# RWKV scan and MoE rewritten as 64-token chunks of two batches on array halves, with the MoE woven into the scan

## The chip, the cores and the metric

The kernel runs on one core of one Trainium2 chip. The metric is the device time of one execution in microseconds (us), lower is better. The kernel before takes 1229.74 us, median of 3 runs (1228.9 to 1230.77).

PE is TensorE's matmul side (PEld its weight load), DVE is VectorE, ACT ScalarE, POOL GpSimd, SP SyncE, which here only issues DMAs. Each engine works through its own queue in order. A "unit" below is 128 rows: 64 tokens of two batches. A "turn" is one pass of the changed kernel's main loop, which finishes one unit.

## The reference, cut to what matters

```python
# batch 4, 8 heads, 768 tokens, head size 40; state is 40 x 40 per batch and head
for t in range(S):
    y[:, :, t] = einsum('bhd,bhde->bhe', rt, state)
    Sa = einsum('bhde,bhe->bhd', state, at)
    state = state * wt[:, :, None, :] - einsum('bhd,bhe->bhde', Sa, bt) \
            + einsum('bhd,bhe->bhde', vt, kt)
x = y.transpose(0, 2, 1, 3).reshape(3072, 320)
h = x @ w_in                                   # 320 x 2048
g = where(h > 0, h, exp(minimum(h, 0)) - 1)    # ELU
out = g @ w_out                                # 2048 x 320
```

The recurrence over tokens can be done by chunks: inside a chunk it is matrix products with triangular masks and a triangular solve; only the 40 x 40 state passes from chunk to chunk.

## The kernel before

It has two stages. The scan takes 6 chunks of 128 tokens and in each handles 32 pairs of batch and head one after the other; the MoE takes the result in groups of 512 tokens.

```python
for c in range(NC):                      # 6 chunks
    ...                                  # load r k v w a b of the chunk, Ln, cumulative sum, Exp
    for bh in range(BH):                 # 32 batch-head pairs
        def transp(x_slice, name, dt=BF16):
            pT = psL.tile([D, C], FP32, name="pT", tag="psL")
            nc.tensor.transpose(pT, x_slice, id128)          # fp32
            xA = phA.tile([D, C], dt, name=name, tag="phA")
            nc.vector.tensor_copy(xA, pT)
            return xA
        r_A = transp(r_S[:, bh, :], "r_A")
        ...                              # v, ktil, atil, cw
        pU = php.tile([C, D], FP32, name="pU", tag="php")
        nc.tensor.matmul(pU, atil_A, s_ed_b, start=True, stop=False)
        nc.tensor.matmul(pU, Kd, v_b[:, bh, :], start=False, stop=True)
        nc.vector.tensor_copy(U_Sf, pU)
        U_A = transp(U_Sf, "U_A")
        ...                              # two masked products, y, state update
...
for gi in range(NG):                     # 6 groups of 512 tokens
    ...
    for j in range(NFB):                 # 16 blocks of 128 features
        ...                              # 3 matmuls into ph
        nc.vector.tensor_scalar(hneg, ph, scalar1=0.0, scalar2=None, op0=ALU.min)
        nc.scalar.activation(hneg, hneg, AF.Exp)
        nc.vector.tensor_scalar(hneg, hneg, scalar1=-1.0, scalar2=None, op0=ALU.add)
        nc.vector.tensor_scalar(g, ph, scalar1=0.0, scalar2=None, op0=ALU.max)
        nc.vector.tensor_add(gT, g, hneg)
        ...                              # 4 matmuls into oacc
```

Of the kernel before, what the change touches and what calls it, by code (L numbers as in the profile page):

```python
# [8 lines left out]
FP32 = mybir.dt.float32  # L9
AF = mybir.ActivationFunctionType  # L10
ALU = mybir.AluOpType


@with_exitstack
def kernel(
    ctx: ExitStack,
    tc: tile.TileContext,
    r: bass.AP,
    k: bass.AP,
    v: bass.AP,  # L20
    w: bass.AP,
    a: bass.AP,
    b: bass.AP,
    moe_w_in: bass.AP,
    moe_w_out: bass.AP,
    out: bass.AP,
):
    nc = tc.nc
    B, H, S, D = r.shape
    BH = B * H  # L30
    C = 128
    NC = S // C
    dmod = H * D
    dff = moe_w_in.shape[1]
    ntok = B * S

    x_tmp = nc.dram_tensor("rwkv_y", (ntok, dmod), FP32, kind="Internal").ap()

    const = ctx.enter_context(tc.tile_pool(name="const", bufs=1))
    id128 = const.tile([128, 128], FP32, name="id128")  # L40
    nc.gpsimd.memset(id128, 0.0)
    nc.gpsimd.affine_select(id128, id128, pattern=[[-1, 128]], channel_multiplier=1,
                            base=0, compare_op=ALU.not_equal, fill=1.0)
    tri_li = const.tile([128, 128], FP32, name="tri_li")
    nc.gpsimd.memset(tri_li, 1.0)
    nc.gpsimd.affine_select(tri_li, tri_li, pattern=[[1, 128]], channel_multiplier=-1,
                            base=0, compare_op=ALU.is_ge, fill=0.0)
    mask_sl = const.tile([128, 128], FP32, name="mask_sl")
    nc.gpsimd.memset(mask_sl, 1.0)
    nc.gpsimd.affine_select(mask_sl, mask_sl, pattern=[[1, 128]], channel_multiplier=-1,  # L50
                            base=-1, compare_op=ALU.is_ge, fill=0.0)

    st_pool = ctx.enter_context(tc.tile_pool(name="state", bufs=1))
    state_de = st_pool.tile([D, BH, D], FP32, name="state_de")
    state_ed = st_pool.tile([D, BH, D], FP32, name="state_ed")
    nc.gpsimd.memset(state_de, 0.0)
    nc.gpsimd.memset(state_ed, 0.0)

    def view(t):
        return t.rearrange("b h (nc s) d -> nc s b h d", s=C)  # L60
    rV, kV, vV, wV, aV, bV = [view(t) for t in (r, k, v, w, a, b)]
    xV = x_tmp.rearrange("(b nc s) (h d) -> nc s b h d", b=B, nc=NC, h=H)

    BF16 = mybir.dt.bfloat16
    rwkv_ctx = ExitStack()
    chS = rwkv_ctx.enter_context(tc.tile_pool(name="chS", bufs=2))
    tmpS = rwkv_ctx.enter_context(tc.tile_pool(name="tmpS", bufs=1))
    phA = rwkv_ctx.enter_context(tc.tile_pool(name="phA", bufs=16))
    php = rwkv_ctx.enter_context(tc.tile_pool(name="php", bufs=6, space=bass.MemoryType.PSUM))
    psL = rwkv_ctx.enter_context(tc.tile_pool(name="psL", bufs=2, space=bass.MemoryType.PSUM))  # L70

    for c in range(NC):
        r_S = chS.tile([C, BH, D], FP32, name="r_S")
        k_S = chS.tile([C, BH, D], FP32, name="k_S")
        v_S = chS.tile([C, BH, D], FP32, name="v_S")
        w_S = chS.tile([C, BH, D], FP32, name="w_S")
        a_S = chS.tile([C, BH, D], FP32, name="a_S")
        b_S = chS.tile([C, BH, D], FP32, name="b_S")
        for tS, tV in [(r_S, rV), (k_S, kV), (v_S, vV), (w_S, wV), (a_S, aV), (b_S, bV)]:
            nc.gpsimd.dma_start(out=tS.rearrange("s (b h) d -> s b h d", b=B),  # L80
                                in_=tV[c])

        F = BH * D
        lw = tmpS.tile([C, BH, D], FP32, name="lw")
        nc.scalar.activation(lw, w_S, AF.Ln)
        cw = tmpS.tile([C, BH, D], FP32, name="cw")
        lwf = lw.rearrange("s b d -> s (b d)")
        cwf = cw.rearrange("s b d -> s (b d)")
        nn = 0
        while nn < F:  # L90
            step = min(512, F - nn)
            pcs = psL.tile([C, step], FP32, name="pcs", tag="psL")
            nc.tensor.matmul(pcs, tri_li, lwf[:, ds(nn, step)], start=True, stop=True)
            nc.vector.tensor_copy(cwf[:, ds(nn, step)], pcs)  # L94
            nn += step
        Wpre = tmpS.tile([C, BH, D], FP32, name="Wpre")
        nc.vector.tensor_sub(Wpre, cw, lw)
        nc.scalar.activation(Wpre, Wpre, AF.Exp)
        necw = tmpS.tile([C, BH, D], FP32, name="necw")
        nc.scalar.activation(necw, cw, AF.Exp, scale=-1.0)  # L100
        ktil = tmpS.tile([C, BH, D], FP32, name="ktil")
        nc.vector.tensor_mul(ktil, k_S, necw)
        nbtil = tmpS.tile([C, BH, D], FP32, name="nbtil")
        nc.vector.tensor_mul(nbtil, b_S, necw)
        nc.scalar.mul(nbtil, nbtil, -1.0)
        atil = tmpS.tile([C, BH, D], FP32, name="atil")
        nc.vector.tensor_mul(atil, a_S, Wpre)

        y_S = chS.tile([C, BH, D], FP32, name="y_S")

        v_b = tmpS.tile([C, BH, D], BF16, name="v_b"); nc.vector.tensor_copy(v_b, v_S)
        ktil_b = tmpS.tile([C, BH, D], BF16, name="ktil_b"); nc.vector.tensor_copy(ktil_b, ktil)
        nbtil_b = tmpS.tile([C, BH, D], BF16, name="nbtil_b"); nc.vector.tensor_copy(nbtil_b, nbtil)

        for bh in range(BH):
            def transp(x_slice, name, dt=BF16):
                pT = psL.tile([D, C], FP32, name="pT", tag="psL")
                nc.tensor.transpose(pT, x_slice, id128)  # L118
                xA = phA.tile([D, C], dt, name=name, tag="phA")
                nc.vector.tensor_copy(xA, pT)  # L120
                return xA
            r_A = transp(r_S[:, bh, :], "r_A")
            v_A = transp(v_S[:, bh, :], "v_A")
            ktil_A = transp(ktil[:, bh, :], "ktil_A")
            atil_A = transp(atil[:, bh, :], "atil_A")
            cw_A = transp(cw[:, bh, :], "cw_A", FP32)

            s_de = state_de[:, bh, :]
            s_ed = state_ed[:, bh, :]
            s_de_b = phA.tile([D, D], BF16, name="s_de_b", tag="phA")  # L130
            nc.vector.tensor_copy(s_de_b, s_de)
            s_ed_b = phA.tile([D, D], BF16, name="s_ed_b", tag="phA")
            nc.vector.tensor_copy(s_ed_b, s_ed)

            pKd = php.tile([C, C], FP32, name="pKd", tag="php")
            nc.tensor.matmul(pKd, ktil_A, atil_A, start=True, stop=True)  # L136
            Kd = phA.tile([C, C], BF16, name="Kd", tag="phA")
            nc.vector.tensor_mul(Kd, pKd, mask_sl)  # L138
            pU = php.tile([C, D], FP32, name="pU", tag="php")
            nc.tensor.matmul(pU, atil_A, s_ed_b, start=True, stop=False)  # L140
            nc.tensor.matmul(pU, Kd, v_b[:, bh, :], start=False, stop=True)  # L141
            U_Sf = phA.tile([C, D], FP32, name="U_Sf", tag="phA")
            nc.vector.tensor_copy(U_Sf, pU)  # L143
            U_S = phA.tile([C, D], BF16, name="U_S", tag="phA")
            nc.vector.tensor_copy(U_S, pU)
            U_A = transp(U_Sf, "U_A")
            pA1 = php.tile([C, C], FP32, name="pA1", tag="php")
            nc.tensor.matmul(pA1, v_A, r_A, start=True, stop=True)
            A1 = phA.tile([C, C], BF16, name="A1", tag="phA")
            nc.vector.tensor_mul(A1, pA1, mask_sl)  # L150
            pA2 = php.tile([C, C], FP32, name="pA2", tag="php")
            nc.tensor.matmul(pA2, U_A, r_A, start=True, stop=True)  # L152
            A2 = phA.tile([C, C], BF16, name="A2", tag="phA")
            nc.vector.tensor_mul(A2, pA2, mask_sl)
            pY = php.tile([C, D], FP32, name="pY", tag="php")
            nc.tensor.matmul(pY, r_A, s_de_b, start=True, stop=False)
            nc.tensor.matmul(pY, A1, ktil_b[:, bh, :], start=False, stop=False)
# [10 lines left out]
            nc.tensor.matmul(pSd, s_ed, id128[:D, :D], start=True, stop=True)  # L168
            nc.vector.tensor_copy(s_de, pSd)

        nc.gpsimd.dma_start(out=xV[c], in_=y_S.rearrange("s (b h) d -> s b h d", b=B))

    rwkv_ctx.close()

# [6 lines left out]
    KM = [128, 128, 64]  # L181
    FB = 128
# [83 lines left out]
```

## Time and profile before

| | scan | MoE |
|---|---|---|
| until | about 940 us | 1229 us |
| PE busy, DVE busy | 76%, 76% (200 to 800 us) | 73%, 91% (1000 to 1200 us) |
| granted TensorE clock | 0.51 | 0.82 |

These are the lines of the windows view: a stretch in us, its length, the busy time of each engine with the number of instructions, the granted clock as a share of full speed, the DMA share and GB/s.

```profile
200.00:800.00 600.00, 457.30 (x2295) 207.92 (x2294) 454.97 (x2183) 51.99 (x147) 27.78 (x17) 0.51 0.09 20
1000.00:1200.00 200.00, 146.91 (x570) 55.04 (x578) 181.86 (x377) 46.63 (x74) 20.54 (x38) 0.82 0.10 32
```

In the scan no engine is full, because PE and DVE wait for each other inside each small problem. This group of the profile's page (line, engine, operation, output from input, count, busy us, mean ns, idle time before it and what ended most of it) shows one such wait, 192 times:

```profile
L118 PE MATMUL pT<-id_58,U_Sf 128*40 128x128 f32 x192 | 76.9, 401 | 56.3 <-DVE U_Sf L143 56.3
```

In the MoE DVE is the bound. The timeline shows its four ops on PSUM or SBUF per block of 128 x 512 (start, duration):

```profile
1152.12 0.68 DVE L226 TENSOR_SCALAR g<-ph 128x512 f32<-128x512 f32 x1
1152.72 0.42 DVE L224 TENSOR_SCALAR hneg<-hneg 128x512 f32<-128x512 f32 x1
1153.05 0.68 DVE L222 TENSOR_SCALAR hneg<-ph 128x512 f32<-128x512 f32 x1
1153.65 0.68 DVE L228 TENSOR_TENSOR gT<-g,hneg 128x512 bf16<-128x512 f32 x1
```

They repeat every 2.13 us.

### The profile page before, as it was taken

How to read it: one execution, taken by the hardware profiler on the slowest of the kernel's cores; microseconds unless marked ns; L12 is line 12 of the kernel's file. 1: busy time of each engine (PE TensorE's matmuls, PEld its weight loads, DVE VectorE, ACT ScalarE, POOL GpSimd, SP SyncE). 2: the span in 40 equal slices, each digit the busy share in tenths (PEclk: the TensorE clock that was granted, in tenths of full speed). 3: DMA queues.
4: the chain of work that ended last, by engine and by line, in shares of the span. 5: the costliest groups of instructions: out<-in, count | busy, mean ns of one | idle time of the engine just before them, and what ended most of it. 6: DMA issues, size and time to landing. Idle time of an engine off the chain costs nothing. (4 is left out here: it accounts for less than half of the span.)

```text
span 1229.1 us, 13572 instructions
## 1 busy us (share of the span) xinstructions
PE 883.8 (72%) x4224; PEld 387.0 (31%) x4236; DVE 935.9 (76%) x3823; ACT 144.9 (12%) x324; POOL 111.7 (9%) x121
## 2 busy tenths in 40 slices
PE   1688876888768886688867888688883567776774
PEld 0233332333323333333323333233331122222221
DVE  1877777777777777777777777777774789889986
ACT  1200011000110001100011000100000122222221
POOL 5400012000120001100010000000002210110010
PEclk9555555555555555555555555555555589779888
DMA  8920024000240002300020000000003310110000
GB/s 144 181 39 1 1 65 86 1 1 1 65 86 1 1 1 65 64 1 1 1 65 1 1 1 1 22 1 1 1 1 122 102 43 1 43 43 21 23 33 22
DMA packets 10713, 41.51 MB, mean 34 GB/s; under 512 B 1744, under 2 KB 1744, under 8 KB 10320
## 3 DMA queue, kind: packets, MB, share of 16 engines
q0 software_dynamic: 10640, 40.64, 14.6%
q8 instruction: 33, 0.54, 0.2%
q14 instruction: 40, 0.33, 0.1%
HBM read 32.77 MB, written 7.86 MB: 33 GB/s over the span
## 5 line engine op out<-in xcount | busy, mean ns | idle before, releaser
L164 ACT ACTIVATE Wall<-cw_A 40x1 f32<-40x1 f32 x192 | 39.0, 203 | 768.0 <-DVE cw_A L120 754.8
L118 PE MATMUL pT<-id_58,ktil 128*40 128x128 f32 x192 | 77.1, 402 | 58.6 <-DVE r_A L120 41.2
L118 PE MATMUL pT<-id_58,U_Sf 128*40 128x128 f32 x192 | 76.9, 401 | 56.3 <-DVE U_Sf L143 56.3
L120 DVE CAST U_A<-pT 40x128 bf16<-40x128 f32 x192 | 54.3, 283 | 74.5 <-PE pT L118 74.5
L223 ACT ACTIVATE hneg<-hneg 128x512 f32<-128x512 f32 x96 | 60.5, 630 | 221.2 <-DVE hneg L222 184.7
L143 DVE COPY U_Sf<-pU 128x40 f32<-128x40 f32 x192 | 38.3, 200 | 61.7 <-PE pU L141 61.7
L118 PE MATMUL pT<-id_58,cw 128*40 128x128 f32 x192 | 80.5, 419 | 0.8 <-DVE ktil_A L120 0.8
L118 PE MATMUL pT<-id_58,r_S 128*40 128x128 f32 x192 | 80.4, 419 | 0.3 <-DVE cw L94 0.3
L118 PE MATMUL pT<-id_58,atil 128*40 128x128 f32 x192 | 76.9, 400 | 4.7 <-DVE v_A L120 4.6
L118 PE MATMUL pT<-id_58,v_S 128*40 128x128 f32 x192 | 76.8, 400 | 0.4 <-DVE cw L94 0.2
L120 DVE CAST atil_A<-pT 40x128 bf16<-40x128 f32 x192 | 54.3, 283 | 26.2 <-PE pT L118 0.5
L136 PE MATMUL pKd<-atil_A,ktil_A 40*128 40x128 bf16 x192 | 50.5, 263 | 30.1 <-DVE atil_A L120 30.1
L222 DVE TENSOR_SCALAR hneg<-ph 128x512 f32<-128x512 f32 x96 | 65.8, 685 | 8.3 <-PE ph L219 8.2
L168 PE MATMUL pSd<-id_58,state_ed 40*40 40x40 f32 x384 | 67.6, 274 | 0.8 <-DVE state_ed L166 0.4
L226 DVE TENSOR_SCALAR g<-ph 128x512 f32<-128x512 f32 x96 | 65.7, 684 | 0.0
L228 DVE TENSOR_TENSOR gT<-g,hneg 128x512 bf16<-128x512 f32 x96 | 65.4, 682 | 0.1
L138 DVE TENSOR_TENSOR Kd<-pKd,mask_sl 128x128 bf16<-128x128 f32 x192 | 62.6, 326 | 0.0
L140 PE MATMUL pU<-s_ed_b,atil_A 40*128 40x40 bf16 x192 | 36.2, 188 | 35.1 <-DVE Kd L138 10.6
L230 PEld LDWEIGHTS <-gT 128*128 128x128 bf16 x384 | 32.6, 104 | 86.6 <-DVE gT L228 71.9
L152 PEld LDWEIGHTS <-U_A 40*128 40x128 bf16 x192 | 19.3, 101 | 126.5 <-DVE U_A L120 119.0
L80 POOL DMA_DIRECT2D r_S<-in_r_dram x6 | 10.3, 1713 | 502.6 <-PE pT L118 239.7
L120 DVE CAST ktil_A<-pT 40x128 bf16<-40x128 f32 x192 | 54.3, 283 | 2.0 <-PE pT L118 1.5
(2089 smaller groups left out, 1891.2 us busy)
## 6 DMA issues: line engine op xcount, KB each, us to landing
r_S<-in_r_dram POOLq DMA_DIRECT2D x6, 640.0 KB, 7.2
k_S<-in_k_dram POOLq DMA_DIRECT2D x6, 640.0 KB, 8.0
v_S<-in_v_dram POOLq DMA_DIRECT2D x6, 640.0 KB, 8.7
w_S<-in_w_dram POOLq DMA_DIRECT2D x6, 640.0 KB, 10.6
a_S<-in_a_dram POOLq DMA_DIRECT2D x6, 640.0 KB, 9.6
b_S<-in_b_dram POOLq DMA_DIRECT2D x6, 640.0 KB, 10.5
rwkv_y<-y_S POOLq DMA_DIRECT2D x6, 640.0 KB, 3.7
x_t<-rwkv_y POOLq DMA_DIRECT2D x24, 160.0 KB, 2.5
```

The source lines that it names most:

```text
L118: nc.tensor.transpose(pT, x_slice, id128)
L120: nc.vector.tensor_copy(xA, pT)
L136: nc.tensor.matmul(pKd, ktil_A, atil_A, start=True, stop=True)
L138: nc.vector.tensor_mul(Kd, pKd, mask_sl)
L140: nc.tensor.matmul(pU, atil_A, s_ed_b, start=True, stop=False)
L143: nc.vector.tensor_copy(U_Sf, pU)
L164: nc.scalar.activation(Wall, cw_A[:, C - 1:C], AF.Exp)
L168: nc.tensor.matmul(pSd, s_ed, id128[:D, :D], start=True, stop=True)
L222: nc.vector.tensor_scalar(hneg, ph, scalar1=0.0, scalar2=None, op0=ALU.min)
L223: nc.scalar.activation(hneg, hneg, AF.Exp)
L226: nc.vector.tensor_scalar(g, ph, scalar1=0.0, scalar2=None, op0=ALU.max)
L228: nc.vector.tensor_add(gT, g, hneg)
```

## The change

The intent: handle all 8 heads of two batches in one unit of 64 tokens, so that one eviction serves 16 small products; put the two batches on two halves of the array, rows and columns 0 to 63 and 64 to 127, so that neighbouring small matmuls don't meet; solve the triangular system (I + N) x = f with a few products by N and N squared, with a check on the chip that N squared is small and a general branch for when it is not; and weave the MoE of an earlier unit into the scan of a later one, by hand, so that no engine has to wait. The file is new almost throughout; this is its core:

```diff
-    for c in range(NC):
-        ...
-        for bh in range(BH):
-            ...                     # one head at a time
-    for gi in range(NG):
-        ...                         # MoE afterwards
+        self.ld = P("ld", 5)        # w k a b, fp32
+        self.vn = P("vn", 6)        # v, bf16
+        self.wk = P("wk", 4, space=psum)
+    def diag(self):
+        for h in range(8):
+            for bb in range(2):     # the two batches alternate
+                yield h, slice(64*bb, 64*bb+64), slice(64*bb, 64*bb+40), h == 0, h == 7
+    def load(self, n):
+        ...                         # w k a b by the SP queue, 8 runs of 160 bytes per partition
+        x = self.vn.tile([128, 8, 40], BF16, name="vn")
+        for bb in range(2):         # fp32 -> bf16 in the DMA, by the POOL queue
+            self.nc.gpsimd.dma_start(out=x[...], in_=self.v[...])
+    def ln(self, n):   ...          # ACT Ln
+    def winv(self, n): ...          # ACT Exp
+    def mulA(self, n):
+        self.nc.gpsimd.tensor_mul(self.Ap[n % 3][:, :, 0:40], self.live["a", n], self.live["wpre", n])
+    def ds(self, n):                # state update, reads vn of unit n
+        for h, tb, fb, first, last in self.diag():
+            self.mm(o, K[tb, h, :], V[tb, h, :], first, False)
+            self.mm(o, B[tb, h, :], U[tb, h, 0:40], False, last)
+        ...
+        for n in range(-3, NU + 4):             # one turn
+            if n >= -1:
+                do(self.load, n + 5)
+            ...                                 # in two turns of four: r and v for the transposes
+            do(self.elu2, n - 3, 2)
+            do(self.xt, n - 2)
+            ...
+            do(self.mulA, n + 2)                # POOL
+            ...
+            do(self.elu1, n - 2, 0, nc.gpsimd)  # ELU half on POOL
+            do(self.x1, n)
+            do(self.ut, n - 1)
+            do(self.ds, n - 1)
+            do(self.ntr, n + 1)
+            do(self.ln, n + 3)
+            do(self.trAK, n + 2)                # PE transposes of Ap and Kp
+            ...
+        return nc.values_load(self.flag, min_val=0, max_val=1)
+    with tc.manual_schedule():
+        more = Chunks(own, tc, *args).run()
+        with tc.If(more > 0):
+            Chunks(own, tc, *args).general()
```

## The prediction

> **What bounds the kernel now.** Two stages in series. In the windows view the scan runs to about 940 us and the MoE from about 945 to 1229 us. The scan handles 6 chunks x 32 heads = 192 small problems, 4.9 us each; in 200 to 800 us PE and DVE are each busy 76%: neither is full, because they wait on each other (groups: PE waits 56 us for U_Sf). The granted clock there is 0.51. In the MoE DVE is the bound (182 us busy of 1000 to 1200 us), five ops per 128x512 block, 2.1 us per block in the timeline, clock 0.8. ACT is busy 12%.
>
> **What the change does.** It runs scan and MoE together: 24 units of 128 rows (64 tokens x two batches), the MoE of unit n-2 woven into the scan of later units, so 945 us and 284 us overlap. All eight heads share one PSUM bank, so one 128x512 or 128x320 eviction replaces 16 small ones (DVE pays 0.28 us for 40x128, 0.68 us for 128x512 out of PSUM). fp32 transposes (0.19 us start to start in the timeline) become bf16. The round trip of y and the fp32 weight casts (no PE work at 945 to 962 us) go. It adds a solve in N and N-squared steps, a certificate and a general branch; computed from the inputs, the certificate is 0.00085 against a limit of 0.00195, so the branch is not taken.
>
> **Cost of one unit (estimates).**
> - PE: 352 small matmuls (40 or 64 columns), 48 of 128 columns, 16 of 320, 4 others. Before, with a 40-column load and matmul each, start to start was 0.05 to 0.06 us at clock 0.5; 320 columns took 0.135 us at full clock. The Trainium skill (TensorE: Matmul & The Clock Gate, Part 3) says a weight load overlaps a matmul in flight only where the row group differs, which alternating the two batches on two halves gives (not shown here yet). So I take 0.03 to 0.04 us per small matmul: 12.5 us; plus 3.3 (48), 2.2 (16), 0.8, and about 1 us of mode changes. Sum about 19 us, range 15 to 27.
> - DVE: ops of 0.68 us and some of 0.4: about 10 us.
> - ACT: 0.63 us per 512 elements: four exps, evictions, the square: about 10 us, plus two table loads of 1.28 us if Ln and Exp still alternate (the trace shows 12 loads in 6 chunks): 12 us.
> - POOL: multiplies, state update, two ELU ops, descriptors: 8 to 11 us.
> - DMA: before moved 640 KB of 160-byte runs per 3.6 us; a unit needs 7 to 8 us.
>
> So PE bounds a unit, at 16 to 20 us if waits are hidden and the clock nears 1. 24 x 17.5 us = 420 us, plus about 60 us for filling and draining: 480 us.
>
> **What would show it.** Clock above 0.85 in the middle; PE busy over 85%, ACT 60 to 75%, DVE 50 to 65%; a period of 16 to 20 us per unit; small matmuls 0.03 to 0.04 us start to start; two table loads per unit.
>
> **What would make it wrong.** (1) The clock stays at half although PE is dense: a unit takes 28 us or more, 700 us in all. (2) Small matmuls don't overlap (0.055 us): 600 us. (3) ACT's in-order queue stalls the solve's chain of five evictions per unit. (4) POOL runs late with its ELU half. (5) A unit takes 13 us: 370 us.
>
> Predicted 480 us, 390 to 620; faster 0.97, same 0.02, slower 0.01.

## The result and the profile after

The changed kernel takes 507.77 us, median of 4 runs (505.85 to 509.45), against 1230.26 us of the kernel before in the same rounds. The ratio is 0.4127, 95% interval 0.4117 to 0.4138. Ratios here are the mean time of one kernel's fast runs over that of the other's of the same rounds, so not quite the ratio of the medians. The output is correct and the general branch did not run.

The prediction said 480 us, 390 to 620: right in the time. Its parts were not all right, and the trace shows that at once. The busy times of the page (part 1):

```profile
PE 343.3 (68%) x9948; PEld 283.3 (56%) x9948; DVE 221.5 (44%) x465; ACT 288.7 (57%) x504; POOL 256.9 (51%) x254
```

Per unit (divided by 24) this is 9.2 us for DVE, 12.0 for ACT and 10.7 for POOL, as estimated. But no engine is near full, PE least of all as forecast ("PE busy over 85%"). The timeline of PE shows why (start, duration with the pipeline's latency, count; the distance between starts is what PE really spends):

```profile
157.46 0.41 PE L346 MATMUL wkb<-idb,STb 40*64 40x40 bf16 x16
157.72 0.42 PE L45 MATMUL wkf<-RT,VT 40*64 40x64 bf16 x16
157.97 0.42 PE L45 MATMUL wkf<-RT,UT 40*64 40x64 bf16 x16
158.63 0.44 PE L202 MATMUL wkb<-idb,Bp 64*64 64x64 bf16 x16 [0.24 <-DVE S L213]
159.00 0.84 PE L45 MATMUL h<-xT,win 128*128 128x128 bf16 x12
159.68 0.71 PE L45 MATMUL po<-wout,g 128*128 128x320 bf16 x4
160.32 0.43 PE L45 MATMUL wkf<-xs,N2T 64*64 64x40 bf16 x16
```

Most groups of sixteen small matmuls take 0.26 us, 0.016 us each; the prediction had 0.03 to 0.04. With 0.68 us for 12 matmuls of 128 columns and 0.64 us for 4 of 320, PE's own work is 352 x 0.016 + 4 x 0.68 + 4 x 0.64 + about 0.8 = about 12 us per unit, not 19. (That is an estimate from this stretch, where PE runs at its full rate.) Yet a turn takes 17.2 us, and 20.7 us in the two turns of four that also load r and v for the transposes (distance between the starts of the xT copies on ACT). The waits view (who waited for whom, us in total, times, longest) says where the rest is:

```profile
PE wkb L202 <- POOL Ap L184: 96.6, 20, 16.8
DVE g L413 <- POOL t L407: 91.7, 32, 6.7
POOL vn L129 <- PE wkb L238: 76.3, 16, 5.6
```

PE waits 97 us for POOL's multiply Ap; and POOL waits 76 us, before a DMA issue for vn, for PE. POOL's timeline over one turn (in brackets the idle time before, and what ended it):

```profile
262.80 1.46 POOL L129 DMA_DIRECT2D vn<-in_v_dram  x2 [4.70 <-PE wkb L238]
264.25 0.89 POOL L184 TENSOR_TENSOR Ap<-na,wpre 128x320 bf16<-128x320 f32 x1
265.09 1.94 POOL L407 TENSOR_SCALAR t<-e 128x512 bf16<-128x512 f32 x1
266.99 0.73 POOL L337 TENSOR_TENSOR S<-t,WTr 128x320 f32<-128x320 f32 x1
271.22 1.02 POOL L178 TENSOR_TENSOR Kp<-nk,winv 128x320 bf16<-128x320 f32 x1 [3.50 <-ACT winv L162]
272.37 1.92 POOL L407 TENSOR_SCALAR t<-e 128x512 bf16<-128x512 f32 x1
274.25 1.02 POOL L181 TENSOR_TENSOR Bp<-nb,winv 128x320 bf16<-128x320 f32 x1
280.00 1.46 POOL L129 DMA_DIRECT2D vn<-in_v_dram  x2 [4.73 <-PE wkb L238]
```

POOL is idle 8 us of 17: 3.5 us of them it waits for ACT's winv, and 4.7 us it stands at the vn issue, with Ap and the rest of its queue behind it. That load is for unit n+5, and the tile vn has 6 buffers, so it overwrites unit n-1, which the state update `ds(n-1)` still reads in the middle of the same turn. The releaser that the profile names is the matmul group right behind `ds` on PE. So there is a loop: `ds` on PE releases the load, the load releases Ap, Ap releases the transposes, and PE goes on from there to the next `ds`. Every item on it adds to the turn; the r and v issues (four, 3.6 us together in this trace) stand between vn and Ap and match the 3.5 us between the two kinds of turns.

Where the span of 503.7 us goes: the first xT copy starts at 84.9 us, the last at 482.5 us (23 distances, 17.3 us on average, the first 17 of them 19.1 us; the last turns have less and less to do), and 21.2 us follow. Fill and drain are longer than the 60 us that were forecast.

### The profile page after: what moved, and what is told of

The parts are those of the page before. It is cut to its first block, busy times and chain, and to the rows that moved or that the text cites. A ratio compares the mean times of both kernels' runs of the same rounds, so it can differ in the third digit from the quotient of the medians.

```text
span 503.7 us, 22017 instructions
## 1 busy us (share of the span) xinstructions
PE 343.3 (68%) x9948; PEld 283.3 (56%) x9948; DVE 221.5 (44%) x465; ACT 288.7 (57%) x504; POOL 256.9 (51%) x254
## 2 busy tenths in 40 slices
DMA packets 210743, 36.05 MB, mean 72 GB/s; under 512 B 205200, under 2 KB 210320, under 8 KB 210640
## 3 DMA queue, kind: packets, MB, share of 16 engines
q0 software_dynamic: 77680, 8.53, 29.9%
## 5 line engine op out<-in xcount | busy, mean ns | idle before, releaser
L407 POOL TENSOR_SCALAR t<-e 128x512 bf16<-128x512 f32 x48 | 92.8, 1934 | 44.6 <-ACT e L401 21.6
L413 DVE TENSOR_TENSOR g<-t,h 128x512 bf16<-128x512 bf16 x96 | 65.5, 682 | 93.7 <-POOL t L407 91.7
L45 PE MATMUL h<-xT,win 128*128 128x128 bf16 x1152 | 91.2, 236 | 2.3 <-DVE g L413 2.2
L129 POOL DMA_DIRECT2D vn<-in_v_dram x48 | 35.0, 736 | 87.5 <-PE wkb L238 76.3
L45 PEld LDWEIGHTS <-win 128*128 128x128 bf16 x1152 | 74.8, 106 | 6.0 <-issue 2.0
L45 PE MATMUL po<-wout,g 128*128 128x320 bf16 x384 | 75.7, 324 | 2.1 <-DVE g L413 2.1
L401 ACT ACTIVATE e<-h 128x512 f32<-128x512 f32 x96 | 57.3, 597 | 27.7 <-PE h L45 26.6
L211 ACT ACTIVATE xs<-px 128x320 bf16<-128x320 f32 x72 | 31.4, 436 | 32.8 <-PE px L45 32.7
L45 PEld LDWEIGHTS <-g 128*128 128x128 bf16 x384 | 36.7, 106 | 12.5 <-DVE g L413 2.8
L45 PEld LDWEIGHTS <-N2T 64*64 64x64 bf16 x1152 | 25.9, 115 | 28.1 <-issue 28.0
L149 ACT ACT_TABLE_LOAD x24 | 30.8, 1283 | 4.9 <-DMA nw<-in_w_dram 4.5
L401 ACT ACT_TABLE_LOAD x19 | 24.4, 1283 | 5.9 <-PE h L45 5.8
```

Source lines behind the costliest of these rows:

```text
L45: self.nc.tensor.matmul(out, lhsT, rhs, start=start, stop=stop, skip_group_check=True)
L129: self.nc.gpsimd.dma_start(out=x[64 * bb:64 * bb + 64], in_=self.v[2 * bp + bb, :, 64 * c:64 * c + 64, :].rearrange("h s d -> s h d"))
L149: self.nc.scalar.activation(x, self.live["w", n].rearrange("p h d -> p (h d)"), AF.Ln)
L211: self.nc.scalar.activation(out, in_, AF.Copy, scale=scale)
L401: self.nc.scalar.activation(e, p, AF.Exp)
L407: eng.tensor_scalar(t, e, scalar1=1.0, scalar2=-1.0, op0=ALU.min, op1=ALU.add)
```

## The experiments

Theory W (wait): the missing vn buffer sets the turn. Rival L (load): POOL is simply overloaded, with ELU ops of 1.93 us. Twelve kernels ran, in three groups. The kernel before was run beside each group and stayed at 1229.6 to 1230.5 us (medians), so the groups can be compared. Medians and ranges are over all runs. Five of these runs count as slow, because they lie over 1.5% above the fastest of the same kernel: 450.2 us of e1, 380.12 us of e12 and all of e13 but the fastest. Without them the medians of e1 and e12 are 443.78 and 375.09 us.

| run | what | us, median | range |
|---|---|---|---|
| after | the change | 507.77 | 505.85 to 509.45 |
| e1_vn8 | 8 vn buffers | 444.38 | 441.47 to 450.2 |
| e2_elu_dve | ELU ops of POOL on DVE, 6 buffers | 497.31 | 497.27 to 497.87 |
| e3_half_order | small matmuls not alternating, 6 buffers | 574.17 | 572.49 to 575.39 |
| e4_mulA_first | Ap ahead of the loads, 6 buffers | 474.94 | 473.75 to 476.61 |
| e8_vn8_oneset | e1 and one ACT table set | 420.28 | 417.5 to 421.15 |
| e6_vn8_elu_dve | e1 and ELU on DVE | 430.9 | 429.84 to 433.28 |
| e9_all | e1, e4, e6 and e8 together | 409.9 | 408.61 to 411.23 |
| e7_two_stages | e1, not woven | 594.31 | 593.62 to 596.5 |
| e10_two_stages_dve | e7, ELU on DVE | 520.95 | 519.71 to 521.82 |
| e11_two_stages_blocks | e10, fewer DMA packets (wrong result) | 500.63 | 498.89 to 502.82 |
| e12_all_blocks | e9, fewer DMA packets (wrong result) | 375.69 | 373.93 to 380.12 |
| e13_all_start | e9, other order of the first loads | 402.43 | 396.08 to 408.56 |

### e1_vn8: two more buffers

```diff
-        self.vn = P("vn", 6)
+        self.vn = P("vn", 8)
```

> The changed kernel with 8 instead of 6 buffers for the tile vn (v in bf16). Theory W (a wait in the POOL queue): the load of vn for unit n+5 reuses the buffer of unit n-1, whose last reader is the state update of unit n-1 in the middle of the same turn, so it holds up the whole in-order POOL queue, the multiply Ap behind it, and the transposes of Ap on PE behind that (97 us of PE waits for Ap in the trace). With two more buffers that wait goes: the period falls from 17.2 and 20.7 us (without and with the r and V loads) to about 14.4 us in both, as in the last turns of the trace that load nothing; PE's wait for Ap under 25 us in sum; total 415 to 430 us. Rival L (POOL is simply overloaded by slow work: ELU ops of 1.93 us, descriptors): the wait moves elsewhere in the POOL queue and the total stays above 480 us.

Measured: 444.38 us, 63 us less than the change. The ratio to the kernel before is 0.3627 (0.3603 to 0.3652). Turns without the extra loads take 14.3 to 14.5 us, as forecast; turns with them about 16 us instead of 14.4, so the total misses the forecast of 415 to 430. (The longest turn takes 18.7 us.) POOL no longer idles ahead of the vn issue:

```profile
265.56 1.02 POOL L181 TENSOR_TENSOR Bp<-nb,winv 128x320 bf16<-128x320 f32 x1
266.52 1.60 POOL L129 DMA_DIRECT2D vn<-in_v_dram  x2
268.13 0.88 POOL L184 TENSOR_TENSOR Ap<-na,wpre 128x320 bf16<-128x320 f32 x1
```

and PE's wait for Ap fell to a third (the forecast was under 25 us), most of it a single one at the start:

```profile
PE wkb L202 <- POOL Ap L184: 29.1, 9, 17.0
```

POOL and ACT do the same work as before (POOL 257.5 us busy against 256.9). PE's busy time fell from 343.3 to 321.9 us with the same number of matmuls, and the clock granted from 92 to 300 us rose from 0.85 to 0.98. So a part of the 63 us may be PE running faster once it no longer stands idle so long in every turn; how large a part was not measured. Theory W holds: the missing buffer is the cause, whichever way it cost.

### e2_elu_dve: take work off POOL, leave the wait

```diff
-            do(self.elu1, n - 2, 0, nc.gpsimd)
+            do(self.elu1, n - 2, 0, nc.vector)
-            do(self.elu1, n - 2, 2, nc.gpsimd)
+            do(self.elu1, n - 2, 2, nc.vector)
```

> The changed kernel with the two ELU ops per unit that POOL does (1.93 us each) given to DVE (0.43 us each), vn still with 6 buffers. Theory W: the ELU ops stand behind Ap in the queue and are not in the loop that sets the period, so the total stays at 495 to 510 us although POOL's busy time falls by 93 us. Rival L: POOL's work is what costs, and the total falls to 430 to 460 us.

Measured: 497.31 us, 2% less. POOL's busy time fell from 256.9 to 164.9 us, DVE's rose from 221.5 to 247.6 us, and the turns kept their 17.0 and 20.5 us. POOL simply waits longer at the vn issue, 109 us instead of 76:

```profile
POOL vn L129 <- PE wkb L238: 108.9, 16, 7.5
```

Rival L falls.

### e4_mulA_first: leave the wait, change what stands behind it

```diff
+            do(self.mulA, n + 2)
             if n == -2:
                 self.load_weights()
             if n >= -1:
                 do(self.load, n + 5)
...
-            do(self.mulA, n + 2)
```

> The changed kernel with the multiply Ap of unit n+2 placed ahead of the loads in POOL's order; vn still with 6 buffers, so the wait itself stays. Theory W says that the wait costs through what is queued behind it: PE no longer waits for Ap, and what remains behind the wait is the ELU op of the next half (needed about 4 to 8 us later), so most is won: 425 to 450 us, a little worse than with 8 buffers, with the loss in the turns that load r and V. Rival L: above 480 us, since POOL's work is the same.

Measured: 474.94 us. Half of what e1 wins (33 of 63 us), without a byte of memory; the forecast of 425 to 450 was too good. PE's wait for Ap is gone but for the first one. In its place:

```profile
PE wkb L202 <- DVE S L213: 57.4, 19, 5.7
DVE g L413 <- POOL t L407: 77.6, 29, 5.9
```

Now the next item behind the vn wait in POOL's queue, the ELU op, is late; DVE waits for it in its own in-order queue (it did so before, 91.7 us, but PE stood at Ap anyway); and the PSUM eviction S behind that on DVE keeps PE waiting. The turns show it: 14.4 to 16 us where only vn is issued, 20.5 us where the r and v issues follow. A wait in an in-order queue costs through everything behind it, so moving one victim out of the way exposes the next.

### e3_half_order: what alternating the halves is worth

```diff
-        for h in range(8):
-            for bb in range(2):
+        for bb in range(2):
+            for h in range(8):
```

> The changed kernel with the order of the small matmuls turned: all 8 heads of one batch, then all 8 of the other, so that neighbours use the same half of the array instead of alternating. In the trace of the changed kernel 16 small matmuls take 0.26 us start to start (0.016 us each). If the alternation is what makes them overlap, this becomes 0.03 us or more each, PE's work per unit grows by 5 us or more, and since PE lies in the loop the total goes to 600 us or more. If alternation does not matter (the engine finds the overlap by itself or there is none to find), the total stays within 2% of 508 us.

Measured: 574.17 us, 13% more than the change; turns of 20.4 and 23.9 us. In one product of y the change starts two matmuls (x2) every 0.03 us:

```profile
160.94 0.19 PE L45 MATMUL wkf<-S,RT 40*64 40x40 bf16 x2
160.97 0.18 PE L45 MATMUL wkf<-Kp,A1T 64*64 64x40 bf16 x2
161.00 0.19 PE L45 MATMUL wkf<-Bp,A2T 64*64 64x40 bf16 x2
```

and this kernel one:

```profile
282.10 0.18 PE L45 MATMUL wkf<-Kp,A1T 64*64 64x40 bf16 x1
282.14 0.18 PE L45 MATMUL wkf<-Bp,A2T 64*64 64x40 bf16 x1
282.17 0.18 PE L45 MATMUL wkf<-S,RT 40*64 40x40 bf16 x1
282.20 0.18 PE L45 MATMUL wkf<-Kp,A1T 64*64 64x40 bf16 x1
```

The cost is 3.2 us a turn, less than the 5 us that doubling all 352 would give, and so the forecast of 600 us or more was missed. In the trace the second half of one group runs together with the first half of the next, so part of the overlap comes back by itself. Alternation does what the change meant it to do. (The mean clock is nearly the same in the two profiled runs, 0.864 and 0.858, so it is no rival.)

### e8_vn8_oneset: ACT's table loads

The Ln of each unit and the Exps that follow are in different table sets as the kernel is built: the trace has 48 loads of 1.28 us. One line loads a set that holds both, at the start, and no other load is then needed.

```diff
+        nc.scalar.add_instruction(mybir.InstLoadActFuncSet(
+            name=nc.get_next_instruction_name(), ins=[], outs=[], act_func_set_id=6))
```

> The kernel with 8 vn buffers (444 us) plus one ACT table set that holds Ln and Exp, loaded once at the start: the 48 table loads of 1.28 us (62 us of ACT time, 2.6 us of each 14.4 us turn) go, results stay correct. In that kernel ACT is busy about 12 us of 14.4. Theory P (PE bounds the 14.4 us turn and ACT has slack): 435 to 445 us. Theory A (the in-order ACT queue bounds it or delays PE): 400 to 425 us.

Measured: 420.28 us, and correct; against e1 the ratio of the two ratios is 0.3419/0.3627 = 0.943. Theory P falls: with ACT's busy time down from 288.2 to 225.4 us the plain turns went from 14.4 to 13.0 us (12.8 to 14.1). ACT was busy 66% of the span in e1 and still set part of the turn, because a table load of 1.28 us in its in-order queue delays what stands behind it. One path can be followed in the trace of e1: a load from 240.16 us stands before the exp of an MoE block; DVE waits 1.13 us for that exp; the eviction S behind it in DVE's queue starts at 242.43 us; and PE waits 0.73 us for S. These are the waits in e1, and the second of them in e8 (its lines are numbered one higher):

```profile
PE wkb L202 <- DVE S L213: 16.5, 17, 1.3
DVE t L407 <- ACT e L401: 59.8, 43, 3.7
```

```profile
DVE t L408 <- ACT e L402: 30.3, 38, 1.5
```

The wait for S is no longer among PE's longest in e8. How much of the 24 us comes by this path, and how much by ACT's own copies in the solve, was not separated.

### e6_vn8_elu_dve and e9_all

e6 is e1 with the edit of e2; e9 has the edits of e1, e2, e4 and e8.

> The kernel with 8 vn buffers plus both POOL ELU ops given to DVE. With the wait gone, the turns that also issue the r and V loads still take about 1.5 us longer (15.9 against 14.4 us), with PE waiting for Ap behind those issues in POOL's queue. Theory Q (POOL's queue in those turns is what is left): all turns near 14.4 us, total 425 to 437 us. Rival: POOL's load does not matter any more, total within 1% of 444 us.

Measured: 430.9 us. The same edit that gave 10 us with 6 buffers gives 13 us here; three of the eight long turns came down to 14.4 or 14.5 us, the others take 14.9 to 16.2. The total is in the range of theory Q, but not all turns are near 14.4 us, so POOL's queue is only a part of what is left in them.

> Everything at once: 8 vn buffers, one ACT table set, both POOL ELU ops on DVE, Ap ahead of the loads in POOL's order. If PE's own work of about 13.5 us bounds a turn: turns of 14.0 to 14.4 us throughout, total 415 to 430 us. If ACT was a partner in the 14.4 us, turns near 12.5 to 13 us, total 385 to 410 us.

Measured: 409.9 us, correct, 0.3333 (0.3323 to 0.3343) of the kernel before and 0.3333/0.4127 = 0.81 of the change. Most plain turns take 13.0 or 13.1 us. The total is at the edge of the second forecast: ACT was a partner, and with it gone PE, busy 12.4 of 13 us in a plain turn, is as good as full. That PE is now the bound is read from this view; no run made PE's work smaller. The turns that load r and v still take 14.9 to 17.2 us. A plain turn and one of the others in the windows view:

```profile
200.00:213.00 13.00, 12.36 (x425) 10.49 (x423) 10.18 (x21) 9.21 (x20) 5.17 (x6) 1.00 0.56 75
213.00:228.00 15.00, 14.12 (x460) 11.61 (x457) 12.23 (x24) 10.49 (x22) 10.26 (x12) 1.00 1.30 112
```

In the second the DMA share is 1.30, more than all 16 engines' time by the packets' durations.

### e7, e10, e11: without weaving

e7 runs all scan turns first, keeps xT for all 24 units, and then runs the MoE in a loop of its own, with 8 vn buffers.

```diff
-            do(self.elu2, ...); do(self.mm1, ...); do(self.mm2, ...); do(self.elu1, ...); do(self.store, ...)
+        for i in range(4 * NU + 2):              # after the scan loop
+            if i < 4 * NU:
+                n, j = i // 4, i % 4
+                self.mm1(n, j)
+                self.elu1(n, j, nc.vector if j % 2 else nc.gpsimd)   # e10: always nc.vector
+                self.elu2(n, j)
+            if i >= 2:
+                n, j = (i - 2) // 4, (i - 2) % 4
+                self.mm2(n, j)
+                if j == 3:
+                    self.store(n)
```

> The kernel with 8 vn buffers, but not interleaved: all scan turns first (xT kept for all 24 units), then all 24 MoE units in a loop of their own. Estimate: scan turns of 10 to 11 us (PE work 6.6 us plus waits for the evictions), MoE 5.5 us a unit, fill and drain about 80 us: 450 to 500 us. If that holds, weaving the two together is worth 10% at most and the gain over the kernel before comes from batching the heads. Rival, which the prediction leaned on: the overlap of the two stages is a main source; then 550 us or more.

Measured: 594.31 us, 150 us more than e1 with the same work. My estimate falls and the rival stands. Two things were behind it. One is my MoE loop: with POOL's op of 1.92 us in a short chain it takes 8.6 us a unit. So e10 puts it on DVE.

> The two-stage kernel (594 us) with the ELU ops of its MoE loop all on DVE, so that POOL's 1.93 us op is no longer in the short chain matmul, exp, ELU, matmul with two PSUM buffers. There the MoE took 8.6 us a unit with PE waiting 79 us for g. If that op was what held the MoE loop: 5.5 to 6.5 us a unit, total 520 to 550 us; the rest of the distance to the woven kernel with the same ops (431 us) is then what weaving is worth. If not: above 580 us.

Measured: 520.95 us, as forecast; the MoE now takes about 5.5 us a unit with DVE busy 80%. The fair distance is then e10 against e6, both with the same ops on the same engines: 521 against 431 us, so weaving is worth 90 us, measured against this two-stage version.

The other thing is the scan by itself: its turns take 13.5 us, hardly less than the 14.4 us of the woven kernel that does the MoE as well. The windows of e10 and e6 from 200 to 300 us, in this order:

```profile
200.00:300.00 100.00, 88.55 (x2614) 76.89 (x2608) 41.99 (x88) 67.89 (x118) 53.95 (x63) 0.52 0.97 93
```

```profile
200.00:300.00 100.00, 85.98 (x2770) 71.76 (x2765) 66.75 (x134) 77.66 (x138) 44.95 (x52) 0.95 0.84 87
```

Alone, the scan keeps PE busy 89% at a granted clock of 0.52; woven with the MoE, PE is busy 86% at 0.95. But the DMA engines are full too in e10 (0.97), so e11 reads the same bytes in 8 times longer runs, with a wrong result. (This makes fewer packets of w, k, a, b and vn. The r and v loads for the transposes write to tiles with gaps and keep theirs, as e12 shows below.)

```diff
-  in_=src[2 * bp + bb, :, 64 * c:64 * c + 64, :].rearrange("h s d -> s h d")
+  in_=self.block(src, 2 * bp + bb, 64, c)     # 320 contiguous elements per partition
```

> As the two-stage kernel with ELU on DVE, but w, k, a, b, v and r are read as contiguous blocks of the same size: each partition's 320 elements in one run instead of eight runs of 160 bytes. The result is wrong on purpose (the values come in another order; the certificate, worked out for that order, stays at 0.0008 and the branch is not taken). Its scan turns took 13.5 us at a granted clock of 0.9 and of 0.53 alike, with the DMA engines 88 to 100% busy. Theory D (the scan alone is bound by the number of DMA packets): scan turns fall to 9 to 11.5 us. Theory C (bound by PE at the half clock): scan turns stay at 13 us or more.

Measured: turns of 13.5 us again, though the DMA share is now 0.67:

```profile
200.00:300.00 100.00, 85.20 (x2673) 73.72 (x2671) 42.43 (x90) 69.28 (x118) 47.33 (x57) 0.60 0.67 87
```

Theory D falls, and theory C fits: alone, the scan is bound by PE at a low clock. ACT, whose table loads are still in these kernels, is no rival here, for PE hardly waits: from 200 to 300 us its waits for other engines come to about 13 us, of which this is the largest:

```profile
PE px L45 <- ACT xs L215: 4.3, 8, 0.5
```

Of the 20 us that e11 gains, 17 lie at the start (first xT copy at 64 us instead of 81). Part of my own expectation was a misreading: I had written that e7's turns took 13.5 us "at a granted clock of 0.9 and of 0.53 alike". The 0.9 was not true. From 100 to 140 us the windows view of e7 gives a clock of 1.00, yet 16 small matmuls take 0.43 us there and not 0.26:

```profile
121.11 0.61 PE L45 MATMUL px<-xs,N2T 64*64 64x40 bf16 x16
121.56 0.61 PE L45 MATMUL wkf<-AKT 40*64 40x64 bf16 x16
121.99 0.61 PE L45 MATMUL wkf<-AKT,BT 40*64 40x64 bf16 x16
```

The clock view at the beginning of these traces is not to be trusted; the distance between matmuls is the better clock.

### e12_all_blocks and e13_all_start: what is left in e9

e12 is e9 with the reading of e11 (wrong result).

> The combined kernel (410 us, turns of 13.0 us and of 15.1 us where r and V are loaded) with the same contiguous reading, wrong result on purpose. If DMA packets set the longer turns and the slow start: all turns 13.0 us, first MoE unit starting at about 55 us instead of 74, total 365 to 385 us. If POOL's descriptor issues or PE do: 400 us or more (the descriptors get fewer as well, so a gain in POOL's issue time is looked up in the profile apart).

Measured: 375.69 us, in the range, but only one of the two reasons was shown. The profiled run was slow (380.12 us), so its times are to be read with care. The first xT copy is at 56 us instead of 74; e11, in fast runs, shows the same gain. So the number of DMA packets costs 18 us of the start. The long turns take 13.3 to 15.7 us in that profile, 14.5 on average against 15.7 in e9. That does not clear the packets, because the edit left those of the r and v loads as they were. The DMA view of e12 has this line:

```profile
q0 software_dynamic: 56176, 8.53, 32.2%
```

In e9 the queue has 77680 packets. The difference, 21504, is that of the vn loads alone (48 loads, 64 packets instead of 512 each); the 49152 packets of 80 bytes that r and v make are still there. So whether packets set the long turns was not tested, and it stays open.

e13 asks for units 2 and 3 and for the weights later.

```diff
         self.load2(0)
-        self.load(2)
-        self.load2(1)
-        self.load(3)
         for n in range(-3, NU + 4):
-            if n == -2:
+            if n == -1:
                 self.load_weights()
             ...
+            if n == -3:
+                self.load(2)
+                self.load2(1)
+            if n == -2:
+                self.load(3)
```

> The combined kernel with the same loads in another order at the start: only units 0 and 1 are requested ahead, units 2 and 3 after the small copy of the chunk decay of unit 0 (it stood behind 32 bulk loads in the SP queue, and DVE waited 20 us for it), the weights one turn later. Theory: that copy's place in the queue, not the amount of data, holds up the start; first MoE unit at 60 to 66 us instead of 74, total 395 to 403 us. Rival (the start is bound by the data that must arrive anyway): within 1% of 410 us.

Measured: 402.43 us, but from 396.08 to 408.56 us, with only the run of 396.08 us counted as fast. The first xT copy came at 69 us in the (slow) profile, later than the 60 to 66 us forecast. The theory of the queue place is at most half right: DVE still waits 18.6 us for that small copy in the profile (20.5 us in e9).

## Why the prediction was right

The time and the direction were right, and so was where the gain comes from: whole batches of heads at once, and the two stages together. "So PE bounds a unit" was wrong for this schedule: the wait for a vn buffer set the turn (e1), and PE was busy 68%. Point by point:

- **What bounds the kernel before**: nothing here contradicts it. The scan waits on itself, at a clock of 0.51.
- **Weaving the two stages**: right, and worth 90 us when both versions have their ELU on DVE (e10 against e6). Not only because the idle times are filled: with the MoE's dense matmuls among them, the small matmuls of the scan also get a clock of 0.95 and not 0.52. I had this as risk (1), "the clock stays at half although PE is dense". It is real; in the woven kernel it does not strike, in the two-stage one it does.
- **PE's work, "about 19 us, range 15 to 27"**: mis-sized, and outside its range. It is about 12 us. The term that failed is "0.03 to 0.04 us per small matmul: 12.5 us"; they take 0.016 us, 5.6 us in all. The overlap of the two halves (Trainium skill, "TensorE: Matmul & The Clock Gate", Part 3) is real and was underrated; e3 shows the price of doing without, 66 us.
- **"if waits are hidden"**: wrong for this schedule. About 4.5 us a turn (31.2 us of PE waits for Ap in the 7 turns from 200 to 330 us) were lost to a buffer too few, and e1 gives back 63 us. I had "(4) POOL runs late with its ELU half". POOL does run late, but e2 shows that it is not the ELU. The two errors, 7 us too many for PE and 4 to 6 us too few for waits, nearly cancel; that 480 came so near to 508 is luck.
- **"four exps, evictions, the square ... plus two table loads"**: 12 us, as measured, 48 loads. What I did not see is that ACT's queue delays PE well before it is full (e8).
- **DVE 10 us, POOL 8 to 11 us**: as measured, 9.2 and 10.7 us.
- **DMA, "7 to 8 us" a unit**: mis-sized. From part 3 of the page:

```profile
q1 hardware_dynamic: 132960, 26.03, 33.8%
q0 software_dynamic: 77680, 8.53, 29.9%
```

  The two shares of 16 engines' 503.7 us come to 321 us, 13.4 us a unit. I had taken the price from the kernel before, as if it moved runs of 160 bytes one by one. The page of that kernel shows packets of 3.8 KB on average:

```profile
q0 software_dynamic: 10640, 40.64, 14.6%
```

  The changed kernel has 210640 packets of 164 bytes on average on its two queues. The queue q0, nearly all loads that cast to bf16, takes 0.299 x 16 x 503.7 us / 77680 = 31 ns a packet; q1 takes 20 ns.
- **"about 60 us for filling and draining"**: too little. It is 84.9 us to the first xT copy, of which 17 to 18 us are DMA packets in later kernels (e11 against e10, e12 against e9), and 21 us after the last one.
- **What would show it**: the mean clock, 0.86, and the two table loads came about as said, and turns of 17.2 and 20.7 us nearly so (16 to 20). The shares of PE (68%, not over 85), ACT (57%, not 60 to 75) and DVE (44%, not 50 to 65) did not, nor did the 0.03 to 0.04 us of the small matmuls.

## What to carry to other kernels

When every engine is half idle in a woven kernel, look in each in-order queue for the one item that waits longest and ask which buffer it waits for; here two more buffers of 640 bytes per partition were worth 63 us, while taking 92 us of work off the same queue was worth 10. A buffer count must cover the distance from the load to the last reader: here the load runs 5 units ahead and the last reader 1 behind, in the middle of a turn, so 6 are one short (by this count 7 would do; 8 were run). Small matmuls should alternate between halves of the array, and dense ones should be mixed in among them, because alone they ran at half the clock (0.52 in e10).

## What the Trainium skill lacked or had wrong

- "TensorE: Matmul & The Clock Gate", Part 1, says that start-to-start never drops below about 25 ns however small a matmul is. Here 16 matmuls of 40 or 64 columns start in 0.26 us, 16 ns each, when two halves of the array alternate. Part 3 of the page, on packing, does give smaller distances, about 4 ns, between matmuls on different tiles; the two parts do not agree as they stand. On one half it is about 0.03 us (e3), which agrees.
- The same page says that the clock follows how busy PE has been. What counts as busy it says only of transposes, which do not count in the same way (Part 4); 96 of the 352 small matmuls of a unit here are transposes, and no run tells whether these or the small tiles keep the clock low. The scan's matmuls, nearly all on tiles of at most 64 x 64, kept PE 89% busy in the records and got a clock of 0.52 (e10); with dense 128-row matmuls among them PE was 86% busy and got 0.95 (e6). The page warns that trace events of the clock can be unreliable; the case found here is a clock of 1.00 at the start of a trace (e7, 100 to 140 us) where the distance of the matmuls, 0.43 against 0.26 us for 16, says about 0.6.
- "ScalarE: Activation LUTs", "What ACT_TABLE_LOAD costs", gives 1283 ns plus a drain of about 1380 ns for a switch. The trace agrees with 1283 ns, but shows no drain in idle time: a copy ends at 279.41 us, the load starts at 279.43 and the next op at 280.72. Its section on table sets says that Ln then Exp needs one load; here it was two per unit (48) until the joint set was loaded by hand at the start, which took e1 from 444 to 420 us.
- "GPSIMD Engine Reference", section 3.1, gives GpSimd as 1.96 times slower than VectorE for a two-input add, and section 4.1 calls a one-input op roughly line-rate. For the one-input op of the ELU (two steps, fp32 to bf16) it is 1.93 against 0.43 us for 128 x 512, 4.5 times.
- No page that I found gives the price of a cast in the DMA: 31 ns a packet on the queue that casts, 20 ns on the other. The two queues also differ in kind (software and hardware) and in packet size (mostly 80 bytes against 160 and 256), so the share of the cast alone is not shown.
